# Storing the pieces of x at different places of a 512-byte row, and the first MLP's matmuls in four forms

## The chip, the cores and the metric

The kernel runs on one core of a Trainium2 chip. The metric is the device time of one execution in microseconds (us), lower is better. The kernel before takes 803.97 us, the median of two runs (803.86 and 804.07).

## What is computed

Retention (attention with a decay in place of the softmax) on 4 x 8 heads of 576 tokens, then two MLPs over 2304 tokens, each 512 wide with a hidden width of 2048:

```python
ret = (scale * q @ k.T) * Dmat          # Dmat[i, j] = gamma ** (i - j) for i >= j, else 0
x   = (ret @ v), heads side by side     # 2304 x 512
h   = np.maximum(x @ w_in, 0.0)         # first MLP
x   = h * h @ w_out
h   = x @ w_in2                         # second MLP
out = (h * np.clip(h + 3.0, 0.0, 6.0) / 6.0) @ w_out2
```

## The kernel before

**Stages.** Retention for the first four 128-token chunks comes first. Then the first MLP runs over five blocks of tokens (512, 384, 512, 384, 512), and the rest of retention is done in between its matmuls. Then the second MLP runs in three super-blocks, each with a stage of matmuls 384 columns wide (z, L1183) and one 256 columns wide (z, L1238).

**Precision.** Each fp32 number is held as two fp32r numbers, a high part and a low part, and each product is made of three matmuls (high by high, high by low, low by high). So `x`, `w` and `g` have an axis of 2: index 0 is the high part, index 1 the low one.

**First MLP.** A step is one of the 16 hidden blocks f of 128 in one block of tokens. `h_part` (L623) does 12 matmuls: the stationary operand is a 128 x 128 piece of `w` (part wi, quarter c of the 512 inputs), the moving one the piece `x[:, xi, c, :]` of as many columns as the block has tokens. ACT then makes relu (L632), DVE multiplies it with h (L634), ACT casts the square to g's high part (L636), DVE subtracts for the low part (L642). `a_part` (L660) does 12 matmuls with pieces of `w` as the stationary and `g` as the moving operand. On PE the order is h of step i+1, then retention's small matmuls if any, then acc of step i. In all these are 588 h matmuls for the 512-token blocks (24 of them 256 columns wide, as step 0 is done in halves), 576 acc matmuls for the same blocks, and 384 of each for the 384-token blocks.

**Weights of the first MLP** are brought in and split during the first block of tokens only, and kept. For each f there are two halves (input weights and output weights). `scale_w` on ACT (L140, L141) and `narrow_w` on DVE (L158, L159) work on the raw 64-bit numbers, whose words they read 8 bytes apart. `cast_w` on ACT (L167) writes w's high part, `low_w` on POOL or DVE (L174) the low part. The high parts are read contiguously and written contiguously.

**Where the tiles lie.** The pools are laid out so that every stationary and moving tile of the first MLP, and `xop` and `ring` of the second, starts 160 bytes into a 512-byte row of its partition; a piece of 128 weights is 512 bytes, and a piece of x or g is 2048 or 1536 bytes, so each piece starts there too. The splits `spl`, the stationary operands of L1238, are the only ones elsewhere: five of six tiles start 224 bytes into the row and the sixth 352, against a moving `ring` at 160.

Of the kernel before, what the change touches and what calls it, by code (L numbers as in the profile page):

```python
# [12 lines left out]
F32R = mybir.dt.float32r  # L13
# [6 lines left out]
P = 128  # L20
B, H, S, D = 4, 8, 576, 64
NT = B * S
DM = H * D
DFF = 2048
NPAIR = H // 2
NC = DM // P
# [9 lines left out]
NJ = NF // 2  # L36
# [50 lines left out]
def retention_moe_kernel(ctx: ExitStack, tc, qk, kv, w1, w2, cst, out):  # L87
# [5 lines left out]
    nc = tc.nc  # L93
    nblk = len(BLOCKS)
    start = np.concatenate([[0], np.cumsum([n for n, _ in BLOCKS])]).tolist()

    def pool(stack, name, bufs, **kw):
        return stack.enter_context(tc.tile_pool(name=name, bufs=bufs, reuse_waits="tile", **kw))
# [7 lines left out]
    whi = pool(left, "whi", 1, side="left")  # L106
# [3 lines left out]
    wlo = pool(right, "wlo", 1, side="right")  # L110
# [7 lines left out]
    ctx.enter_context(tc.manual_schedule())  # L118


    raws = {}
    wts = {}
    narrowed = [0]
# [38 lines left out]
    def cast_w(ph, f, halves=(0, 1)):  # L162

        for i in halves:
            t = wts[ph, f, i]
            w = (wlo if f < NJ else whi).tile([P, 2, DM], F32R, tag=f"w{f}_{i}", name=f"w_{ph}_{f}_{i}")
            nc.scalar.activation(w[:, 0, :], t, AF.Copy)  # L167
            wts[ph, f, i] = w, t

# [7 lines left out]
    def split_w(ph, f, halves=(0, 1)):  # L177
        cast_w(ph, f, halves)
        low_w(ph, f, halves)
# [19 lines left out]
    xs = {}  # L199
# [411 lines left out]
    def h_part(ph, blk, f, between=lambda: None):  # L611
        nb = BLOCKS[blk][0]
        w = wts[ph, f, 0]
        x = xs[ph, blk]
        hp = ps_h.tile([P, 512], F32, tag="h", name=f"h_{ph}_{blk}_{f}")
        def order(last):
            return [(c, wi, xi) for wi, xi in ((0, 0), last[::-1], last) for c in range(NC)]

        parts = 2 if ph == blk == f == 0 else 1
        for i in range(parts):  # L620
            ts = slice(i * nb // parts, (i + 1) * nb // parts)
            for k, (c, wi, xi) in enumerate(order((1, 0) if blk == 0 and i == 0 else (0, 1))):
                nc.tensor.matmul(  # L623
                    hp[:, ts],
                    w[:, wi, c * P : (c + 1) * P],
                    x[:, xi, c, ts],
                    start=k == 0,
                    stop=k == 3 * NC - 1,
                )
        r = tmpp.tile([P, 512], F32, tag="tmp", name=f"r_{ph}_{blk}_{f}")  # L630
        r = r[:, :nb]
        nc.scalar.activation(r, hp[:, :nb], AF.Relu)  # L632
        between()
        nc.vector.tensor_tensor(r, r, hp[:, :nb], ALU.mult)  # L634
        g = gpool.tile([P, 2, 512], F32R, tag="g", name=f"g_{ph}_{blk}_{f}")
        nc.scalar.activation(g[:, 0, :nb], r, AF.Copy)  # L636
        gts[ph, blk, f] = g, r
# [7 lines left out]
    def a_part(ph, blk, f):  # L645
        nb = BLOCKS[blk][0]
        w = wts[ph, f, 1]
        g = gts.pop((ph, blk, f))
        if f == 0:
            two = [  # L650
                ps_acc.tile([P, 2, 512], F32, tag="acc", name=f"acc_{ph}_{blk}_{d}")
                for d in range(2)
            ]
            accs[ph, blk] = [two[d // 2][:, d % 2, :] for d in range(NC)]
        acc = accs[ph, blk]
        last = f == NF - 1

        def mm(d, wi, gi, first, stop):
            wt = w[:, wi, d * P : (d + 1) * P]
            nc.tensor.matmul(acc[d][:, :nb], wt, g[:, gi, :nb], start=first, stop=stop)  # L660

        if last:
            for d in range(NC):
                mm(d, 0, 0, False, False)
                mm(d, 1, 0, False, False)
                mm(d, 0, 1, False, True)
        else:
            for d in range(NC):
                mm(d, 0, 0, f == 0, False)
                mm(d, 1, 0, False, False)  # L670
            for d in range(NC):
                mm(d, 0, 1, False, False)
# [23 lines left out]
    def new_x(ph, blk):  # L696
        nb, tag = BLOCKS[blk]
        p = xbpool if tag == "xb" else xapool
        xs[ph, blk] = p.tile([P, 2, NC, nb], F32R, tag=tag, name=f"x_{ph}_{blk}")

# [159 lines left out]
    for f in range(2, 4):  # L862
        load_w(0, f)
    nc.sync.dma_start(con, cst[:, DK0:])
    new_x(0, 0)

    first_q(0, nc.vector)
# [29 lines left out]
    narrow_w(0, 0, (0,))  # L897
    scale_w(0, 1, (0,))
    cast_w(0, 0, (0,))
    first_x(2, low=True)  # L900
    first_values(3)
# [5 lines left out]
    for i in range(2):  # L907
        first_x(3, i, 2, low=True)
    cast_w(0, 1, (0,))
    scale_w(0, 0, (1,))  # L910
    low_w(0, 1, (0,))
# [3 lines left out]
    def early_between():  # L915
        narrow_w(0, 0, (1,))
        split_w(0, 0, (1,))

    h_part(0, 0, 0, early_between)
    narrow_w(0, 2, (0,))  # L920
    g_low(0, 0, 0)
# [44 lines left out]
    for i, (ph, blk, f) in enumerate(steps):  # L966
# [13 lines left out]
        if i + 1 < len(steps):  # L980
            h_part(*steps[i + 1], lambda: first_between(f) if blk == 0 else None)
            if i == 0:
                narrow_w(0, 1, (1,))
            if blk == 0 and f + 1 < NF:
                cast_w(0, f + 1, (1,))
            if i == 0:
                g_low(*steps[1])
                low_w(0, 1, (1,), nc.vector)
                scale_w(0, 3, (0,))
                first_sum(n0 - 1)  # L990
                scale_w(0, 2, (1,))
            if blk == 0 and f:
                scale_ahead(f, False)
# [11 lines left out]
        if blk + 1 < nblk:  # L1005
            if f == 0:
                new_x(0, blk + 1)
# [153 lines left out]
    for s in range(SUPERS):  # L1161
# [8 lines left out]
        for j in range(NJ):  # L1170
# [5 lines left out]
            for i, q in enumerate(ORDER):  # L1176
                run(now)
                w = wring[s, 0, j, i // 2][:, i % 2]
                x = x_ops[q]
                for k, (u, wi, xi) in enumerate(  # L1180
# [6 lines left out]
                        start=k == 0 and q not in (2, 4, 3),  # L1187
                        stop=k == 5,
# [35 lines left out]
        for i, q in enumerate(ORDER):  # L1224
# [7 lines left out]
            for k, parts in work:  # L1232
                run(now)
                w, sp = wring[s, 1, q, k // 2], splits[s, q, k]
                for n in parts:
                    o = z[A_BANKS[q][n // 2]][:, HALFD * (n % 2) : HALFD * (n % 2 + 1)]
                    for m, (g, wi) in enumerate(((0, 0), (0, 1), (1, 0))):
# [4 lines left out]
                            start=k == 0 and m == 0 and n % 2 == 0 and q not in (2, 4, 3),  # L1242
                            stop=k == NJ - 1 and m == 2 and n > 0,
# [49 lines left out]
```

## Time and profile before

| what | value |
|---|---|
| median of the two runs | 803.97 us |
| span of the profiled execution | 802.6 us |
| TensorE (PE) busy | 796.4 us, 99% |
| weight loads (PEld) busy | 741.0 us, 92% |
| VectorE (DVE) busy | 591.9 us, 74% |
| ScalarE (ACT) busy | 397.5 us, 50% |
| GpSimd (POOL) busy | 167.7 us, 21% |
| DMA share | 73.5% of 16 engines |

The profiled execution is known by its span, 802.6 us from its first to its last instruction; the two timed runs are other executions, whose median is 1.4 us above that span. A matmul's duration in the profile holds both its columns and the time until its last result is written, so durations of matmuls in a stream overlap. The time that one costs is the distance between the starts of two that follow each other, called the pitch here.

### The profile page before, as it was taken

To read this page: it belongs to the slowest core of one execution; us is meant where nothing else is said; L and a number is where in the kernel's file an instruction comes from. 1 tells how busy PE (TensorE), PEld (TensorE's weight loads), DVE (VectorE), ACT (ScalarE), POOL (GpSimd) and SP (SyncE) were. 2 spreads that over 40 slices of the span, in tenths; PEclk is the share of its full clock that TensorE was granted. 3 is DMA by queue.
4 is the path that set the end of the run, shared out by engine and by line. 5 is a ranking of instruction groups with operands and counts; after the bars stand their busy time and mean duration, and the time that the engine had idled before them with its cause. 6 is when DMAs were issued, how large, how long until landed. Compare 5 with 4: busy or idle time off the path is not lost.

```text
span 802.6 us, 16522 instructions
## 1 busy us (share of the span) xinstructions
PE 796.4 (99%) x6380; PEld 741.0 (92%) x6380; DVE 591.9 (74%) x1086; ACT 397.5 (50%) x738; POOL 167.7 (21%) x161
## 2 busy tenths in 40 slices
PE   8999999999999999999999999999999999999998
PEld 8788889999888899998888899999999999999998
DVE  5989987887755577776557867997577987677864
ACT  2797745444443444444435533666234655244553
POOL 4412130211011011100000065500255500256300
PEclk9999999999999999999999999999999999999999
DMA  9957626777756487856448797888887979877884
GB/s 331 352 189 248 223 93 203 225 214 222 222 157 184 124 260 212 234 158 184 145 130 269 242 303 256 306 307 291 274 264 242 353 261 302 279 240 266 272 274 139
DMA packets 148494, 189.64 MB, mean 236 GB/s; under 512 B 22592, under 2 KB 102080, under 8 KB 148416
## 3 DMA queue, kind: packets, MB, share of 16 engines
q1 hardware_dynamic: 148416, 188.59, 73.5%
q8 instruction: 50, 0.82, 0.4%
q14 instruction: 28, 0.23, 0.1%
HBM read 149.76 MB, written 38.80 MB: 235 GB/s over the span
## 4 chain that ended last, share of the span: by engine, by line
PE 95%; DMA 3%; DVE 1%; SPq 0%; ACT 0%; issue 0%; DVEq 0%
PE acc L660 24%; PE h L623 24%; PE z L1183 22%; PE z L1238 21%; PE at L496 2%; DMA raw<-w_dram 1%; DMA v<-kv_dram 1%; DMA kv<-kv_dram 1%; PE alone L496 0%; PE sc L408 0%; PE o L459 0%; PE sc L419 0%; DVE wt L158 0%; DVE wt L159 0%; PE o L469 0%; ACT w L167 0%
## 5 line engine op out<-in xcount | busy, mean ns | idle before, releaser
L660 PE MATMUL acc<-g,w 128*128 128x512 f32 (+1 forms) x960 | 213.3, 370 | 0.4 <-ACT g L636 0.4
L623 PE MATMUL h<-x,w 128*128 128x512 f32 (+2 forms) x972 | 210.6, 365 | 0.2 <-ACT w L167 0.2
L660 PEld LDWEIGHTS acc<-g,w 128*128 128x128 f32 x960 | 173.6, 188 | 25.2 <-ACT g L636 0.8
L623 PEld LDWEIGHTS h<-x,w 128*128 128x128 f32 x972 | 175.7, 188 | 22.8 <-ACT w L167 0.6
L1183 PE MATMUL z<-xop,ring 128*128 128x384 f32 x1008 | 175.2, 334 | 0.0
L1183 PEld LDWEIGHTS z<-xop,ring 128*128 128x128 f32 x1008 | 174.7, 188 | 0.1
L1238 PE MATMUL z<-ring,spl 128*128 128x256 f32 x1512 | 172.2, 276 | 0.0
L1238 PEld LDWEIGHTS z<-ring,spl 128*128 128x128 f32 x1512 | 172.1, 188 | 0.0
L1099 POOL TENSOR_TENSOR aop<-aop,aop 128x384 f32<-128x384 f32 x96 | 106.2, 1116 | 296.2 <-DVE aop L1096 292.4
L1121 DVE TENSOR_TENSOR spl<-aop,spl 128x384 fp32r<-128x384 f32 x168 | 100.5, 617 | 30.7 <-ACT spl L1117 29.4
L1117 ACT ACTIVATE spl<-aop 128x384 fp32r<-128x384 f32 x168 | 86.3, 523 | 54.7 <-PE z L1238 49.8
L632 ACT ACTIVATE r<-h 128x512 f32<-128x512 f32 (+1 forms) x80 | 44.3, 553 | 110.7 <-PE h L623 110.4
L1093 ACT ACTIVATE aop<-held,small 128x384 f32<-128x384 f32 x72 | 44.4, 617 | 108.4 <-DVE held L1059 107.8
L634 DVE TENSOR_TENSOR r<-r,h 128x512 f32<-128x512 f32 (+1 forms) x80 | 50.5, 632 | 53.9 <-ACT r L632 53.5
L1059 DVE TENSOR_TENSOR held<-z,held 128x384 f32<-128x384 f32 x120 | 66.4, 553 | 28.9 <-PE z L1183 26.7
L636 ACT ACTIVATE g<-r 128x512 fp32r<-128x512 f32 (+1 forms) x80 | 47.2, 590 | 65.8 <-DVE r L634 65.8
L642 DVE TENSOR_TENSOR g<-r,g 128x512 fp32r<-128x512 f32 (+1 forms) x80 | 54.7, 684 | 21.0 <-ACT g L636 18.5
L1096 DVE SCALAR_TENSOR_TENSOR aop<-aop,held 128x384 f32<-128x384 f32 x72 | 49.9, 692 | 17.7 <-ACT aop L1093 16.1
L393 POOL TENSOR_TENSOR qs<-qs,con 128x512 f32<-128x512 f32 x11 | 14.7, 1340 | 136.3 <-DMA qs<-qk_dram 123.9
L750 ACT ACTIVATE uhi<-seven 128x896 fp32r<-128x896 f32 x32 | 30.6, 955 | 23.7 <-DVE seven L740 14.0
L755 DVE TENSOR_TENSOR seven<-seven,uhi 128x896 fp32r<-128x896 f32 x32 | 34.9, 1089 | 7.3 <-ACT uhi L750 7.0
L174 POOL TENSOR_TENSOR w<-wt,w 128x512 fp32r<-128x512 f32 x17 | 22.7, 1336 | 62.9 <-ACT w L167 60.2
(111 smaller groups left out, 609.8 us busy)
## 6 DMA issues: line engine op xcount, KB each, us to landing
ring<-w_out_hl SPq DMA_DIRECT2D x84, 512.0 KB, 4.9
ring<-w_in_hl SPq DMA_DIRECT2D x72, 512.0 KB, 4.7
raw<-w_dram SPq DMA_DIRECT2D x32, 512.0 KB, 7.1
uraw<-w_dram SPq DMA_DIRECT2D x64, 256.0 KB, 3.2
q<-qk_dram SPq DMA_DIRECT2D x17, 512.0 KB, 5.3
w_in_hl<-uhi SPq DMA_DIRECT2D x16, 448.0 KB, 3.4
w_in_hl<-seven SPq DMA_DIRECT2D x16, 448.0 KB, 4.8
w_out_hl<-uhi SPq DMA_DIRECT2D x16, 448.0 KB, 3.2
```

Source lines behind the costliest of these rows:

```text
L623: nc.tensor.matmul(hp[:, ts], w[:, wi, c * P : (c + 1) * P], x[:, xi, c, ts], start=k == 0, stop=k == 3 * NC - 1,)
L634: nc.vector.tensor_tensor(r, r, hp[:, :nb], ALU.mult)
L636: nc.scalar.activation(g[:, 0, :nb], r, AF.Copy)
L642: nc.vector.tensor_tensor(g[:, 1, :nb], r, g[:, 0, :nb].bitcast(F32), ALU.subtract)
L660: nc.tensor.matmul(acc[d][:, :nb], wt, g[:, gi, :nb], start=first, stop=stop)
L1059: fn(*a)
L1096: stt(f32(q, j), f32(q, j), 6.0, h, ALU.min, ALU.mult)
L1099: nc.gpsimd.tensor_tensor(f32(o, j), f32(a, j), f32(b, j), op)
L1117: act(t[:, 0, :], f32(q, k), AF.Copy)
L1121: tt(t[:, 1, :], f32(q, k), t[:, 0, :].bitcast(F32), ALU.subtract)
L1183: nc.tensor.matmul(bank[q], w[:, wi, u * P : (u + 1) * P], x[:, u, xi, :], start=k == 0 and q not in (2, 4, 3), stop=k == 5, skip_group_ch ...
L1238: nc.tensor.matmul(o, sp[:, g, P * n : P * (n + 1)], w[:, k % 2, wi, :], start=k == 0 and m == 0 and n % 2 == 0 and q not in (2, 4, 3), st ...
```

## The change

Three things, all in the first MLP; the number of instructions, the work of each and their order on each of the five engines stay the same.

- `new_x`: the x tile of a 512-token block gets rows of 528 elements of which 512 are used. Piece (xi, c) then starts 160 + 64 c + 256 xi bytes into the 512-byte row, modulo 512: 160, 224, 288, 352 for the high parts and 416, 480, 32, 96 for the low ones. Of the 12 h matmuls of a step, the two with (xi, c) = (0, 0) still start where their weights do, the other ten don't. The x tiles of 384-token blocks and the g tiles stay. The tiles behind x move by 512 bytes, so their place in the row stays.
- `woven`: for f = 4 to 7 and 12 to 15, w's high and low parts lie alternately, so a part's 128 weights are 8 bytes apart and span 1024 bytes. The cast, the subtraction and the weight loads of these f work with that step.
- `backwards`: for f = 2, 3, 6, 7, 10, 11, 14, 15, the moving operand is read from its last column to its first, in both `h_part` and `a_part`: h comes out with its tokens in reverse, g inherits that, and the second reversal puts acc right.

So four f each are plain (0, 1, 8, 9), backwards (2, 3, 10, 11), woven (4, 5, 12, 13), and both (6, 7, 14, 15).

```diff
+    def woven(f):
+        return f // 4 % 2 == 1
+
+    def backwards(f):
+        return f // 2 % 2 == 1
+
+    def turned(ap, yes):
+        return ap[:, ::-1] if yes else ap
...
-            w = (wlo if f < NJ else whi).tile([P, 2, DM], F32R, tag=f"w{f}_{i}", name=f"w_{ph}_{f}_{i}")
+            p, name = wlo if f < NJ else whi, f"w_{ph}_{f}_{i}"
+            if woven(f):
+                w = p.tile([P, DM, 2], F32R, tag=f"w{f}_{i}", name=name).rearrange("p n t -> p t n")
+            else:
+                w = p.tile([P, 2, DM], F32R, tag=f"w{f}_{i}", name=name)
...
-                    x[:, xi, c, ts],
+                    turned(x[:, xi, c, ts], backwards(f)),
...
-            nc.tensor.matmul(acc[d][:, :nb], wt, g[:, gi, :nb], start=first, stop=stop)
+            gt = turned(g[:, gi, :nb], backwards(f))
+            nc.tensor.matmul(acc[d][:, :nb], wt, gt, start=first, stop=stop)
...
-        xs[ph, blk] = p.tile([P, 2, NC, nb], F32R, tag=tag, name=f"x_{ph}_{blk}")
+        step = nb + 16 * (tag == "xa")
+        x = p.tile([P, 2, NC, step], F32R, tag=tag, name=f"x_{ph}_{blk}")
+        xs[ph, blk] = x[:, :, :, :nb]
```

## Rows read from the trace of the kernel before

**Rows 1.** The page: busy time and share of PE; its granted clock by slice.
```profile
PE 796.4 (99%) x6380; PEld 741.0 (92%) x6380; DVE 591.9 (74%) x1086; ACT 397.5 (50%) x738; POOL 167.7 (21%) x161
...
PEclk9999999999999999999999999999999999999999
```

**Rows 2.** The page: the chain that ended last, shares by engine.
```profile
PE 95%; DMA 3%; DVE 1%; SPq 0%; ACT 0%; issue 0%; DVEq 0%
```

**Rows 3.** Waits of PE: who waited for whom, us in total, times, longest.
```profile
PE unread L851 <- POOL early L845: 1.0, 1, 1.0
...
PE h L623 <- ACT w L167: 0.2, 1, 0.2
```

**Rows 4.** Groups by shape: line, engine, tiles, shapes, count | busy us, mean ns.
```profile
L1238 PE MATMUL z<-ring,spl 128*128 128x256 f32 x1512 | 172.2, 276 | 0.0
L660 PE MATMUL acc<-g,w 128*128 128x512 f32 x576 | 140.4, 392 | 0.4 <-ACT g L636 0.4
L623 PE MATMUL h<-x,w 128*128 128x512 f32 x564 | 135.8, 390 | 0.2 <-ACT w L167 0.2
L660 PE MATMUL acc<-g,w 128*128 128x384 f32 x384 | 72.9, 337 | 0.0
L623 PE MATMUL h<-x,w 128*128 128x384 f32 x384 | 71.8, 334 | 0.0
```

**Rows 5.** Timeline of PE in steady stretches: start us, length us, matmuls merged.
```profile
215.44 2.88 PE L660 MATMUL acc<-g,w 128*128 128x512 f32 x12
218.16 2.88 PE L623 MATMUL h<-x,w 128*128 128x512 f32 x12
...
125.13 2.24 PE L660 MATMUL acc<-g,w 128*128 128x384 f32 x12
127.21 2.25 PE L623 MATMUL h<-x,w 128*128 128x384 f32 x12
```

**Rows 6.** Timeline of PE: two stretches of 256-wide matmuls.
```profile
22.91 2.92 PE L623 MATMUL h<-x,w 128*128 128x256 f32 x23
...
529.80 15.46 PE L1238 MATMUL z<-ring,spl 128*128 128x256 f32 x135
```

**Rows 7.** One matmul and one weight load in 23.1:25.6; mean ns last.
```profile
L623 PE MATMUL h<-x,w 128*128 128x256 f32 x23 | 2.9, 283 | 0.0
...
L623 PEld LDWEIGHTS h<-x,w 128*128 128x128 f32 x23 | 2.8, 192 | 0.0
```

**Rows 8.** Weight loads by shape, whole span, 128 and 64 columns wide.
```profile
L1238 PEld LDWEIGHTS z<-ring,spl 128*128 128x128 f32 x1512 | 172.1, 188 | 0.0
L496 PEld LDWEIGHTS alone<-p,v 64*64 64x64 f32 x176 | 6.0, 135 | 0.0
```

**Rows 9.** Groups by shape on ACT, DVE and POOL: the weights' preparation.
```profile
L140 ACT ACTIVATE raw<-raw 128x512 f32<-128x512 f32 x32 | 21.3, 666 | 1.0 <-DMA raw<-w_dram 1.0
L167 ACT ACTIVATE w<-wt 128x512 fp32r<-128x512 f32 x32 | 19.9, 623 | 4.0 <-DVE wt L159 3.9
...
L642 DVE TENSOR_TENSOR g<-r,g 128x512 fp32r<-128x512 f32 x48 | 34.5, 719 | 11.6 <-ACT g L636 9.1 <-PE alone L496 1.4 <-PE at L496 0.7
L174 DVE TENSOR_TENSOR w<-wt,w 128x512 fp32r<-128x512 f32 x15 | 11.1, 740 | 0.1
...
L174 POOL TENSOR_TENSOR w<-wt,w 128x512 fp32r<-128x512 f32 x17 | 22.7, 1336 | 62.9 <-ACT w L167 60.2 <-issue 2.7
```

**Rows 10.** Timeline of the first block around one step's weights, several engines.
```profile
96.48 2.88 PE L660 MATMUL acc<-g,w 128*128 128x512 f32 x12
...
97.17 0.62 ACT L167 ACTIVATE w<-wt 128x512 fp32r<-128x512 f32 x1
...
97.87 1.30 POOL L174 TENSOR_TENSOR w<-wt,w 128x512 fp32r<-128x512 f32 x1 [5.04 <-ACT w L167]
...
99.20 2.88 PE L623 MATMUL h<-x,w 128*128 128x512 f32 x12
...
100.45 0.68 DVE L174 TENSOR_TENSOR w<-wt,w 128x512 fp32r<-128x512 f32 x1
...
103.10 0.50 PE L660 MATMUL acc<-g,w 128*128 128x512 f32 x1
```

**Rows 11.** Busy time by stretch, first block: us, PE, PEld, DVE, ACT, POOL.
```profile
36.00:118.00 82.00, 81.80 (x737) 66.34 (x736) 72.68 (x126) 61.57 (x112) 21.76 (x18) 1.00 0.60 202
```

## Prediction

> **What bounds the kernel now.** I read the page's busy shares first, then the chain, then PE's waits, to see whether anything but PE counts. [...] The chain that ended last is PE's for 95% [rows 2]. PE's longest wait is 1.0 us and its shortest listed 0.2 us, six waits in all, 2.7 us together [rows 3]. So the time is the number of matmuls times the pitch of one, and an edit counts only if it changes a pitch or makes PE wait.
>
> So I read the pitches in steady stretches. For 512 columns, twelve acc matmuls start at 215.44 and the h matmuls behind them at 218.16 [rows 5]: 2.72 / 12 = 0.2267 us. The columns alone, at 2.4 GHz, are 512 / 2.4 = 213.3 ns, so 13.3 ns are lost per matmul. For 384 columns it is (127.21 - 125.13) / 12 = 173.3 ns [rows 5] against 160.0: again 13.3 ns. The loss does not depend on the width, so it belongs to the change from one matmul to the next.
>
> The rows that matter most are two stretches of the same shape, 128 x 128 weights against 256 columns [rows 6]. From a stretch I take off the last matmul's own duration, 283 or 276 ns [rows 7, 4], and divide by the starts that are left. In the first block, L623: (2.92 - 0.283) / 22 = 119.9 ns. In the second MLP, L1238: (15.46 - 0.276) / 134 = 113.3 ns. The columns are 106.7 ns in both, so one loses 13.2 and the other 6.6. A weight load lasts 192 ns in the first and 188 in the second [rows 7, 8]. What differs between the two in the kernel is the place in the 512-byte row: in L623 weights and moving operand start at the same byte, in L1238 64 or 192 bytes apart. That is what the change tries on h. The trace does not prove that the place is the cause, since the two lines also write PSUM differently, but every matmul of the first MLP, whose tiles lie at many different places and have only the place in the row in common, has the 13.3 ns.
>
> **The change, part by part.**
>
> *x's pieces.* It touches 564 + 24 = 588 h matmuls [rows 4] (the 24 are in the first step), of which 10 in 12 = 490 no longer start where their weights do. The saving of one lies between nothing and 13.3 ns, all that a 512-column matmul loses. I take 6.6 ns, the difference of the two 256-wide stretches, since it is the only row of before with starts apart. 490 x 0.0066 = 3.2 us; the bounds are 0 and 6.5 us. A loss is not excluded either, as only distances of 64 and 192 bytes have a row and the change makes seven; I bound it by the same 3.2 us the other way.
>
> [...]
>
> *Backwards.* 960 matmuls: 288 h and 288 acc of 512 columns, 192 and 192 of 384. No row shows an operand read backwards. The bounds are a loss of 13.3 ns that vanishes (12.8 us gained) and columns at half speed (below). I take nothing: the same bytes are read, and the row's traffic is the same. *Woven.* Also 960 matmuls, half of which are backwards too. The weight loads read 8 bytes apart, which no row shows on PE either. A load takes 188 ns for 128 columns and 135 for 64 [rows 8], so 53 for 64 columns, 0.83 ns each, and 106.7 for 128; the rest is latency. It lies beside a matmul whose pitch is 227 or 173 ns, so a load that is no more than 1.5 times as slow costs nothing. I take nothing, with bounds from 12.8 us gained to the rival below.
>
> *Preparing woven weights,* first block only. 16 casts on ACT and 16 subtractions on POOL and DVE write (and read) 8 bytes apart. For ACT the near rows are L140, which reads and writes at that step, 666 ns, against L167's 623 [rows 9]: 16 x 43 ns = 0.7 us on an engine that is busy 61.6 of 82 us there [rows 11]. For L174 no row has the step with two inputs; between no change and a doubling I take no change. What hides it: the POOL subtraction ends at 97.87 + 1.30 = 99.17, and the h step that starts at 99.20 wants the low weights only in its last four matmuls, 8 x 0.227 = 1.8 us later; the DVE one ends at 101.13 and its acc step starts at 103.10 [rows 10]. A doubled subtraction (1.3 and 0.7 us more) still fits. Queued behind on DVE are the next narrowings, and DVE is busy 72.7 of 82 us [rows 11]; 8 x 0.7 = 5.6 us more would fit there too, with PE waits of a few tenths.
>
> *Nothing is moved:* each engine's instructions stand in the order of before, and no wait is added.
>
> **Sum.** The profiled span 802.6 - 3.2 = 799.4 us; with the 1.4 us that the median of the runs lies above it, 800.8 us. [...]
>
> **Rivals.**
>
> *The forms shed the loss too.* If what costs is that both streams go through the row in step, then any form that breaks the step saves 6.6 ns in the matmuls without an offset: in three forms of four, 432 + 288 acc, 288 h of 384 columns and 72 h of 512, 1080 x 0.0066 = 7.1 us more: 793.7. For it: the loss is the same in all plain matmuls with equal starts. Against it: nothing shows which direction or step would help.
>
> *The forms make it worse by one meeting.* Streams that run against each other meet more often. One more loss of 6.6 ns in the 960 backward matmuls is 6.3 us: 807.1. No row speaks for or against.
>
> *The change does nothing,* 804.0: the loss is a fixed cost of changing weights, and L1238 is shorter for another reason. For it: 13.3 ns at 512 and 384 columns alike. Against it: the 256-wide stretches. [...]
>
> *Woven loads at half speed.* A load would read for 213 ns instead of 107, and with the 6.6 ns between loads of L1238 no matmul could follow another in under 220 ns. 512-column matmuls at 226.7 hide that; 384-column ones at 173.3 don't: half of 768 x 46.6 ns = 17.9 us, and about 1 us where a load follows a wait and is not hidden: 800.8 + 18.9 = 819.7. It decides from the point where a load takes 173 ns or more to read. [...]
>
> *Backward columns at half speed,* the slower side. Place: the moving operand of 960 matmuls on PE. Price: 576 x 213.3 + 384 x 160.0 ns = 184 us, 985 us. It passes 2% (16.1 us, beyond the 3.2 gained) once a backward matmul takes 20 ns longer. For it: no moving operand of before runs backwards. Against it: only the direction changes, the numbers read and their places are the same.
>
> **Chances.** Offset helps, forms neutral: 0.42. Forms shed the loss too: 0.13. Forms worse by one meeting: 0.15. Nothing: 0.12. Woven loads slow: 0.10. Backward slow: 0.08. The predicted time is that of the likeliest, 800.8 us; its own range is 797 to 804, from the bounds of x's pieces (6.5 and 0 us). The whole range is 793 to 821, from the forms that shed to the slow woven loads; it leaves out the slow columns (0.08) and tails of the others, some 0.15. About 2% is what a measurement of this kernel can tell from no change. Faster by over 2%, under 787.9, needs nearly all of the loss gone in the forms: 0.04, out of the second case. Slower by over 2%, over 820.0: the slow columns (0.08), half of the slow loads, which end close to that bound (0.05), and 0.04 for meetings that cost several times 6.6 ns: 0.17. Within 2%: 0.79.
>
> **What would show it.** Pitches by step in a 512-token block: plain h steps at about 12 x 0.221 = 2.66 us in place of 2.72, acc steps of f = 0, 1, 8, 9 still 2.72. For each form, the acc steps and the 384-column steps tell its own price without x's offset. Woven loads at half speed would show as weight loads near 295 ns in place of 188; slow columns as durations near 600 ns in place of 390. If h steps of all f stay at 2.72, x's pieces do nothing. The forecast is wrong if any form moves the pitch of its acc steps by more than about 7 ns either way, or if PE's waits in the first block grow beyond a microsecond.

## The result and the profile after

The changed kernel takes 812.49 us (two runs, 812.38 and 812.60) against 803.97: a ratio of 1.0107, with a 95% interval of 1.0077 to 1.0136. It is slower, where 800.8 us and a small gain were forecast; it lies within the 2% that most of the chance was on. The profiled execution's span is 810.6 us against 802.6, 8.0 us more.

The page after, parts 1 and 2, which answer to [rows 1]:

```profile
PE 803.7 (99%) x6380; PEld 747.1 (92%) x6380; DVE 591.9 (73%) x1086; ACT 399.7 (49%) x738; POOL 169.3 (21%) x161
...
PEclk9999999999999999999999999999999999999999
```

PE is as full as before and its clock as high, so the time has not gone into waiting or into the clock: PE is busy 7.3 us longer with the same 6380 matmuls. The groups by shape on PE and its weight loads, after (columns as in [rows 4]); h is now L636, acc L674, and the second MLP's stages are L1199 and L1254:

```profile
L1199 PE MATMUL z<-xop,ring 128*128 128x384 f32 x1008 | 175.2, 334 | 0.0
L1254 PE MATMUL z<-ring,spl 128*128 128x256 f32 x1512 | 172.2, 276 | 0.0
L674 PE MATMUL acc<-g,w 128*128 128x512 f32 x576 | 143.2, 398 | 0.4 <-ACT g L649 0.4
L636 PE MATMUL h<-x,w 128*128 128x512 f32 x564 | 139.0, 396 | 0.2 <-ACT w L180 0.2
L674 PE MATMUL acc<-g,w 128*128 128x384 f32 x384 | 73.6, 341 | 0.0
L636 PE MATMUL h<-x,w 128*128 128x384 f32 x384 | 72.7, 338 | 0.0
...
L636 PEld LDWEIGHTS h<-x,w 128*128 128x128 f32 x972 | 178.7, 192 | 23.7 <-ACT w L180 0.6
```

Beside [rows 4], acc of 512 columns went from 140.4 to 143.2 us, h from 135.8 to 139.0, acc of 384 from 72.9 to 73.6 and h from 71.8 to 72.7. That is 2.8 + 3.2 + 0.7 + 0.9 = 7.6 of the 8.0 us. The second MLP, which the change doesn't touch, is the same to a tenth. Weight loads last 192 ns in the mean against 188; those of woven f last 195 ns and none over 201, so none is at half speed.

The steps one by one, in the chain of work of the third block (512 columns); columns are start us, length us, and 12 matmuls of a step. They are h of f = 3 (backwards), acc of f = 2, h of f = 4 (woven), and further down h of f = 9, acc of f = 8 and acc of f = 9, all plain:

```profile
216.06 2.80 PE h L636 x12
218.87 2.80 PE acc L674 x12
221.67 2.78 PE h L636 x12
...
251.86 2.79 PE h L636 x12
254.64 2.73 PE acc L674 x12
...
260.18 2.77 PE acc L674 x12
```

Before, each such step was 2.72 us [rows 5]. Only the plain acc steps, whose code is that of before, still come close: 2.73 behind a plain h step, 2.77 behind a backward one. A plain h step, which has nothing new but x's offset, takes 2.79 in place of the 2.66 that was forecast: 232.5 ns per matmul, not 221. A backward acc step, which has no offset, takes 2.80: 233.3 ns.

### The profile page after: what moved, and what is told of

Read it like the earlier page. It is cut to its first block, busy times and chain, and to the rows that moved or that the text cites. A ratio compares the mean times of both kernels' runs of the same rounds, so it can differ in the third digit from the quotient of the medians.

```text
span 810.6 us, 16522 instructions
## 1 busy us (share of the span) xinstructions
PE 803.7 (99%) x6380; PEld 747.1 (92%) x6380; DVE 591.9 (73%) x1086; ACT 399.7 (49%) x738; POOL 169.3 (21%) x161
## 4 chain that ended last, share of the span: by engine, by line
PE 95%; DMA 2%; DVE 2%; ACT 1%; issue 0%; SPq 0%; POOL 0%; DVEq 0%; POOLq 0%
PE acc L674 25%; PE h L636 24%; PE z L1199 22%; PE z L1254 21%; PE at L509 2%; DMA q<-qk_dram 2%; DVE wt L167 1%; PE alone L509 0%; DVE wt L168 0%; PE sc L421 0%; ACT w L180 0%; PE o L472 0%; PE sc L432 0%; SPq L243 0%; PE o L482 0%
## 5 line engine op out<-in xcount | busy, mean ns | idle before, releaser
L674 PE MATMUL acc<-g,w 128*128 128x512 f32 (+1 forms) x960 | 216.8, 375 | 0.4 <-ACT g L649 0.4
L636 PE MATMUL h<-x,w 128*128 128x512 f32 (+2 forms) x972 | 214.7, 370 | 0.2 <-ACT w L180 0.2
L636 PEld LDWEIGHTS h<-x,w 128*128 128x128 f32 x972 | 178.7, 192 | 23.7 <-ACT w L180 0.6
L674 PEld LDWEIGHTS acc<-g,w 128*128 128x128 f32 x960 | 176.8, 192 | 25.4 <-ACT g L649 0.8
L1199 PE MATMUL z<-xop,ring 128*128 128x384 f32 x1008 | 175.2, 334 | 0.0
L1199 PEld LDWEIGHTS z<-xop,ring 128*128 128x128 f32 x1008 | 174.7, 188 | 0.1
L1254 PE MATMUL z<-ring,spl 128*128 128x256 f32 x1512 | 172.2, 276 | 0.0
L1254 PEld LDWEIGHTS z<-ring,spl 128*128 128x128 f32 x1512 | 172.1, 188 | 0.0
L1115 POOL TENSOR_TENSOR aop<-aop,aop 128x384 f32<-128x384 f32 x96 | 108.0, 1135 | 296.7 <-DVE aop L1112 292.9
L1137 DVE TENSOR_TENSOR spl<-aop,spl 128x384 fp32r<-128x384 f32 x168 | 98.6, 604 | 31.1 <-ACT spl L1133 29.0
```

The costliest lines, as they stand in the source:

```text
L636: nc.tensor.matmul(hp[:, ts], w[:, wi, c * P : (c + 1) * P], turned(x[:, xi, c, ts], backwards(f)), start=k == 0, stop=k == 3 * NC - 1,)
L674: nc.tensor.matmul(acc[d][:, :nb], wt, gt, start=first, stop=stop)
L1115: nc.gpsimd.tensor_tensor(f32(o, j), f32(a, j), f32(b, j), op)
L1137: tt(t[:, 1, :], f32(q, k), t[:, 0, :].bitcast(F32), ALU.subtract)
L1199: nc.tensor.matmul(bank[q], w[:, wi, u * P : (u + 1) * P], x[:, u, xi, :], start=k == 0 and q not in (2, 4, 3), stop=k == 5, skip_group_ch ...
L1254: nc.tensor.matmul(o, sp[:, g, P * n : P * (n + 1)], w[:, k % 2, wi, :], start=k == 0 and m == 0 and n % 2 == 0 and q not in (2, 4, 3), st ...
```

## The experiments

Times are medians, set against the kernel before on the same chip (804.4 to 804.5 us; the two runs of the last part are single executions, read for their pitches alone). A pitch is the length of a stretch in the chain of work divided by its matmuls.

### Each part alone

The theory that the profile after suggests: a stream of wide matmuls has one state that repeats from matmul to matmul at 13.3 ns above its columns, and each of the three parts breaks it by itself. "State" is a name for what the starts show, and for nothing inside the engine. The columns are counted here and below at 2.4 to a ns, an estimate from [rows 5]: 128 columns more take 226.7 - 173.3 = 53.4 ns. The rival: the offset saves as forecast, and the parts only cost together.

**The offset alone.** The diff is that of `new_x` in the change, without the rest.

> The kernel before with the x tiles of the 512-token blocks in rows of 528 alone: no f is read backwards, no weights are woven. In the changed kernel the plain h steps of 512 columns went from 226.7 to about 232.5 ns per matmul. Theory A, unequal starts of the moving pieces are by themselves a loss: all 588 h matmuls at 231 to 234 ns, acc and 384-column matmuls as before, time about 804.0 + 588 x 0.0055 = 807.2 us. Theory B, the offset saves 6.6 ns each as predicted and the forms beside it spoiled the plain steps: h at about 221 ns, 800.8 us.

Measured: 807.84 us, a ratio of 1.0044 (1.0029 to 1.0059), 3.5 us slower. The chain in the third block:

```profile
228.12 2.74 PE acc L660 x12
230.86 2.79 PE h L623 x12
```

The h steps are at 2.79 us, and the acc steps, which are untouched, come to 2.74, 0.02 above before. The offset is a loss of some 6 ns per matmul where a gain of 6.6 was forecast.

**Backwards alone.** With `backwards` and `turned` of the change:

```diff
-                    x[:, xi, c, ts],
+                    turned(x[:, xi, c, ts], backwards(f)),
...
-            nc.tensor.matmul(acc[d][:, :nb], wt, g[:, gi, :nb], start=first, stop=stop)
+            gt = turned(g[:, gi, :nb], backwards(f))
+            nc.tensor.matmul(acc[d][:, :nb], wt, gt, start=first, stop=stop)
```

> The kernel before with the moving operands of f = 2, 3, 6, 7, 10, 11, 14, 15 read backwards alone: x's rows stay 512 long, no weights are woven. Theory A, a backward stream costs by itself: as in the changed kernel, 576 matmuls of 512 columns at about 233 ns (3.6 us) and 384 of 384 columns at about 178 ns (1.7 us), 809.3 us. Theory B, the forms cost only through x's offset: 804 us.

Measured: 809.88 us, 1.0067 (1.0052 to 1.0082), 5.5 us slower. The chain where the second block (384 columns) goes over into the third; h is L632, acc L670:

```profile
194.66 2.13 PE acc L670 x12
196.79 2.73 PE h L632 x12
...
204.40 2.72 PE acc L670 x12
207.12 2.80 PE h L632 x12
```

The first row is acc of f = 14, backwards, 384 columns: 2.13 us in place of 2.08 (4.3 ns per matmul in the mean of such steps). The next are 512 columns: h and acc of f = 0, both forward, at 2.73 and 2.72, and the first backward one, h of f = 2, at 2.80.

**Woven alone.** With `woven` of the change:

```diff
-            w = (wlo if f < NJ else whi).tile([P, 2, DM], F32R, tag=f"w{f}_{i}", name=f"w_{ph}_{f}_{i}")
+            p, name = wlo if f < NJ else whi, f"w_{ph}_{f}_{i}"
+            if woven(f):
+                w = p.tile([P, DM, 2], F32R, tag=f"w{f}_{i}", name=name).rearrange("p n t -> p t n")
+            else:
+                w = p.tile([P, 2, DM], F32R, tag=f"w{f}_{i}", name=name)
```

> The kernel before with the weights of f = 4 to 7 and 12 to 15 woven alone. Theory A, the step of 8 bytes costs by itself but only beside 512 columns: 576 matmuls at about 233 ns, the 384-column ones at 173.3, 804.0 + 3.6 = 807.6 us; the sum of the three parts alone is then larger than the changed kernel's 8.5 us, since the forms overlap. Theory B, it costs nothing without x's offset: 804 us.

Measured: 808.17 us, 1.0045 (1.0028 to 1.0061), 3.8 us slower. The chain in the third block, acc of f = 2 (plain) and h of f = 4 (woven):

```profile
217.06 2.72 PE acc L673 x12
219.79 2.80 PE h L636 x12
```

576 matmuls of 512 columns at 2.80 / 12 = 233.3 ns are 576 x 6.7 = 3.8 us, all of it; the groups of 384 columns stay as before (72.0 and 72.8 us busy).

The three losses sum to 12.8 us and the change costs 8.5. That fits parts that break the same state: an h matmul that has the offset and goes backwards pays some 6 ns once, not twice. In the change 588 h and 432 acc matmuls of 512 columns are out of the state, 1020 x 6 ns = 6.1 us, and 384 backward ones of 384 columns, 384 x 4.3 ns = 1.7 us: 7.8 us. The 72 plain acc matmuls of f = 1 and 9, whose steps stand behind a backward h step, add 72 x 4 ns = 0.3 us.

### Was the place of the splits the cause of the 113.4 ns?

```diff
-    SHIFT, FIRST_SHIFT = 64 // 4, 192 // 4
+    SHIFT, FIRST_SHIFT = 512 // 4, 0
...
-    p1a.tile([P, 128 - SHIFT], F32, tag="shift1", name="shift1")
```

> The kernel before with the splits of the second MLP, the stationary operands of its 256-column matmuls, at the same place of the 512-byte row as the moving ring tiles (160) in place of 224 and 352. Theory A, which the prediction rested on, that the distance of the starts sets the loss: 1512 matmuls go from 113.4 to 119.9 ns, 804.0 + 10 = 814 us. Theory B, the 113.4 ns belongs to that stage for another reason: 804 us.

Measured: 813.92 us, 1.0119 (1.0104 to 1.0134), 9.5 us slower. Pieces of the chain, whole stages of the second MLP's first super-block. Before:

```profile
452.82 58.27 PE z L1183 x336
511.09 57.18 PE z L1238 x504
```

In this run:

```profile
452.61 58.26 PE z L1183 x336
510.87 60.47 PE z L1238 x504
```

60.47 / 504 = 120.0 ns, where the stage had 57.18 / 504 = 113.5. So the inference from [rows 6] held: in the 256-column stage the place of the stationary operand sets the loss, and this alone is worth 9.5 us. In this run nothing but the place of the splits was changed, and each matmul takes 6.5 ns longer. Whether the load takes reads from the matmul, this run doesn't tell.

### Does a constant distance help wide matmuls?

The offset gave x's pieces seven distances in turn. Two runs give the first MLP's weights one constant distance instead, by a tile of padding ahead of them (the first run's edit; the second has 448 and 256 in place of 192 and 64):

```diff
+    whi.tile([P, 192 // 4], F32, tag="whi_shift", name="whi_shift")
...
+    wlo.tile([P, 64 // 4], F32, tag="wlo_shift", name="wlo_shift")
```

> The kernel before with the first MLP's weights moved within the 512-byte row, x and g left at 160: weights of f = 0 to 7 start 64 bytes later (224), those of f = 8 to 15 192 bytes later (352), the two distances that the second MLP's 256-column stage has. Every matmul of the first MLP has then unequal but constant starts. Theory A, what counts is that starts are constant from matmul to matmul, and a distance of 64 or 192 then saves: 512 columns at about 220 ns, 384 at about 167, 1932 x 6.6 ns = 12.8 us less, 791 us. Theory B, equal starts are the best state for wide matmuls and the distance helps only at 256 columns, where the weight loads fill the whole pitch: 512 columns at 231 to 234 ns, about 804 + 1140 x 0.006 = 811 us or more.

> As the run before it, with weights of f = 0 to 7 256 bytes later in the row than x and g, and of f = 8 to 15 448 bytes later (64 earlier). Theory A, any constant distance saves: 791 us. Theory B, equal starts are best for wide matmuls: 811 us or more. If one half of the f shows another pitch than the other, the distance itself matters, and which one is read from the stretches.

Measured: 808.63 us (1.0051, 1.0031 to 1.0071) with 64 and 192 bytes; 805.78 us (1.0014, 1.0004 to 1.0024) with 256 and 448. The chain in the third block, first with 64 bytes (f under 8), then 192:

```profile
228.35 2.80 PE acc L663 x12
...
263.86 2.75 PE acc L663 x12
```

and with 256 bytes, then 448:

```profile
227.69 2.72 PE acc L663 x12
...
262.75 2.75 PE acc L663 x12
```

So 233.3 ns at 64 bytes, 229.2 at 192 and 448, and 226.7, the value of equal starts, at 256. No distance gets below equal starts, so theory A falls in both runs. Theory B has the direction right but its 811 us is too much, as it put the same loss on every distance. In the 384-column blocks of both runs the distances cost next to nothing: the 768 matmuls are busy 145.3 and 144.7 us, where they were 144.7 before [rows 4]. Nor does a distance of 64 bytes help in the second MLP's 384-column stage, where xop was moved by a padding tile ahead of it:

```diff
+        p.tile([P, 448 // 4], F32, tag="xshift", name="xshift")
         for q in ORDER:
             x_ops[q] = p.tile([P, 2, 2, HALF], F32R, tag=f"x{q}", name=f"xop_{q}")
+        p.tile([P, (512 - 448) // 4], F32, tag="xrest", name="xrest")
```

> The kernel before with xop, the moving operand of the second MLP's 384-column stage, 64 bytes earlier in the row than ring, its stationary operand (96 against 160), the same distance as in the 256-column stage. Theory A, a constant distance saves there too: 1008 matmuls from 173.3 to 166.7 ns, 797.3 us. Theory B, equal starts are the best state for matmuls wider than 256 columns: 173.3 stays or rises by some 4 ns, as it did for backward ones, 804 to 809 us.

Measured: 805.98 us, 1.0017 (1.0007 to 1.0027). That stage, L1185 here:

```profile
452.73 58.69 PE z L1185 x336
```

58.69 / 336 = 174.7 ns, in place of 58.27 / 336 = 173.4. Two things are told apart with that: it is not the change of distance from piece to piece alone that costs, since constant ones cost too; and the gain from a distance of 64 bytes belongs to 256 columns.

Does the place itself count, apart from the distance? All tiles 32 bytes later:

```diff
+    cpool.tile([P, 8], F32, tag="by32", name="by32")
...
-    pool(ctx, "align", 1, side="right").tile([P, 80], F32, tag="align", name="align")
+    pool(ctx, "align", 1, side="right").tile([P, 72], F32, tag="align", name="align")
```

> The kernel before with all tiles on both sides 32 bytes later, so that the streams start at 192 in place of 160 bytes into the 512-byte row, a multiple of 64; all distances stay. Theory A, only distances count: 804 us with every pitch as before. Theory B, the 13.3 ns is partly a piece of 64 bytes that is begun in its middle: the pitches of 512 and 384 columns fall by 6.7 ns or less, down to about 787 us with the second MLP's 384-column stage.

Measured: 804.44 us, 1.0002 (0.9992 to 1.0012), and the steps of 512 columns stay at 2.72 us. So moving everything by 32 bytes changes nothing; with what stands above, the distance counts and the place, as far as tried, does not.

And is it 256 bytes that the places repeat by? x's low parts 256 bytes further, so that the moving starts change within each h step:

```diff
-        xs[ph, blk] = p.tile([P, 2, NC, nb], F32R, tag=tag, name=f"x_{ph}_{blk}")
+        rest = 64 * (tag == "xa")
+        x = p.tile([P, 2, NC * nb + rest], F32R, tag=tag, name=f"x_{ph}_{blk}")
+        xs[ph, blk] = x[:, :, : NC * nb].rearrange("p t (c n) -> p t c n", c=NC)
```

> The kernel before with the low parts of x in the 512-token blocks 256 bytes further in the row than the high parts (416 against 160), nothing else: the starts of h's moving pieces change within a step, as in the change, but by 256 bytes in place of 64. Theory A, places count modulo 256 bytes: h stays at 226.7 ns and the time at 804 us. Theory B, any change of place from one moving piece to the next spoils the repeating state: h at 231 to 234 ns in part of its matmuls, 805 to 807 us.

Measured: 804.35 us, 0.9998 (0.9989 to 1.0008). The same kind of edit as the change's, with 256 bytes in place of 64, costs nothing; h and acc in the third block:

```profile
224.07 2.72 PE h L623 x12
226.79 2.72 PE acc L660 x12
```

So of the ten matmuls in twelve that no longer start where their weights do, the one with (xi, c) = (1, 0), 256 bytes off, counts as not moved.

### The matmul by itself

Two runs carry a tail of stretches of 48 matmuls, each with one thing changed. In the tails DVE, ACT and POOL do nothing, DMA's share is 0.00 and the granted clock 1.00. For instance, weights 64 bytes further (`cut` takes a tile, the byte to start at, the step in elements and the number of elements):

```diff
+    for k in range(48):  # d64
+        nc.tensor.matmul(z[5 - k % 2][:128, :512], cut(pw, 64, 1, 128), cut(px[k % 2], 0 + 0 * k % 512, 1, 512), start=True, stop=True)
```

> The kernel before with a tail that measures: behind the second MLP, 25 stretches of 48 matmuls each on tiles of xop, one thing changed at a time, their sums read by nobody (the tail adds some 260 us and is no part of what is computed). Base: 512 columns, 128 weights, equal starts. Theory A, the loss comes from the weight load's reads meeting the moving operand's: it follows the number of weights, 13.3 ns with 128, about 6.7 with 64 and 3.3 with 32, and the start distances and directions change it as in the stages (starts 64 or 192 bytes apart: 229 to 234 ns in place of 226.7; 256 apart: 226.7; moving backwards and woven weights: 233; moving pieces that go on by 64 bytes each: 232; 256 columns: 120 with equal starts, 113.3 with 64 apart). Theory B, it is a fixed price of changing the weights: 13.3 ns with 64 and 32 weights too.

> The kernel before with another tail of 26 stretches of 48 matmuls whose sums nobody reads (some 280 us, no part of what is computed). It asks three things. First, whether the backward stretch's 233.3 ns at 512 columns is its direction or its place, since reading from the last column starts 4 bytes short of the weights' place. Theory A, the place: backward from byte 2048 of the tile (equal places) gives 226.7 ns, and forward with weights 4 or 252 bytes off gives about 233. Theory B, the direction: backward gives about 233 from every start, and 4 bytes forward change nothing. Second, why 256 columns with starts 64 bytes apart give 113.4 ns in the second MLP and 117.7 in the tail of the run before: if the PSUM bank is what differs, 256 columns into one bank, or three in a row into each, give 113.3 and alternating banks 117.7; if the moving tile is, one tile in place of two gives 113.3. Third, whether the loss is 13.3 ns for widths that are no multiple of 128: 504, 496, 480, 448 and 416 columns at N / 2.4 + 13.3, that is 223.3, 220.0, 213.3, 200.0 and 186.7 ns, or more where such a width spoils the repeating state.

The first tail's chain; columns are start us, length us, line, and 48 matmuls. In order: equal starts, 64 weights, 32 weights, distances of 16, (32 left out, 11.20,) 64, 128, 192, 256 bytes (those of 320, 384 and 448, L1285 to L1289, are left out: 11.20, 11.16 and 10.99), backwards, woven. A distance is how far the weights start behind the moving operand:

```profile
803.33 10.98 PE z L1267 x48
814.31 11.04 PE z L1269 x48
825.35 11.12 PE z L1271 x48
836.47 11.20 PE z L1273 x48
...
858.87 11.20 PE z L1277 x48
870.07 11.15 PE z L1279 x48
881.22 10.99 PE z L1281 x48
892.21 10.88 PE z L1283 x48
...
936.45 11.20 PE z L1291 x48
947.64 11.20 PE z L1293 x48
958.84 11.28 PE z L1295 x48
970.12 21.75 PE z L1297 x48
991.87 11.13 PE z L1299 x48
1003.00 10.89 PE z L1301 x48
1013.90 5.75 PE z L1303 x48
...
1025.30 5.45 PE z L1307 x48
...
1055.92 10.89 PE z L1315 x48
```

L1295 is weights 16 bytes apart, L1297 moving numbers 8 bytes apart, L1299 moving pieces that go on by 64 bytes, L1301 by 256. L1303 is 256 columns with equal starts, L1307 the same with 64 weights, and L1315 is the first form once more. The second tail's chain: L1281 is the backward stretch that starts at the weights' place (four others are left out, 11.31 each), L1291 to L1295 are 496, 480 and 504 columns, L1309 is 256 columns with the weights 64 bytes off and one moving tile:

```profile
880.41 11.30 PE z L1281 x48
...
936.94 10.72 PE z L1291 x48
947.66 10.41 PE z L1293 x48
958.08 10.88 PE z L1295 x48
...
1009.94 5.44 PE z L1309 x48
```

Divided by 48, in ns per matmul of 512 columns unless said:

| what is changed | pitch | over the columns |
|---|---|---|
| equal starts (L1315); 256 bytes apart; pieces that go on by 256 | 226.7 to 226.9 | 13.3 to 13.5 |
| 192 or 448 apart | 229.0 | 15.7 |
| 240, 8 and 96 apart (second tail: 10.97, 11.07 and 11.24 us) | 228.5, 230.6, 234.2 | 15.2, 17.3, 20.8 |
| 4 apart (L1269 of the second tail, 11.16 us) | 232.5 | 19.2 |
| 128 or 384 apart; pieces that go on by 64 | 231.9 to 232.5 | 18.6 to 19.2 |
| 16, 32, 64, 224, 252 or 320 apart; backwards from 4 bytes short; woven | 233.3 | 20.0 |
| backwards from the weights' place and four other starts | 235.4 to 235.6 | 22 |
| weights with a step of 16 bytes | 235.0 | 21.7 |
| 64 weights, 32 weights, equal starts | 230.0, 231.7 | 16.7, 18.3 |
| 504, 496, 480 columns, equal starts | 226.7, 223.3, 216.9 | 16.7, 16.6, 16.9 |
| 448, 416 columns, equal starts (9.72 and 9.04 us) | 202.5, 188.3 | 15.8, 15.0 |
| 384 columns: equal starts; 64 weights; backwards (8.32, 8.32, 8.53 us) | 173.3, 173.3, 177.7 | 13.3, 13.3, 17.7 |
| 256 columns, equal starts: 128 weights; 64 weights | 119.8, 113.5 | 13.1, 6.9 |
| 256 columns, 64 or 192 apart; 32 apart, two moving tiles (5.65, 5.68 us) | 117.7, 118.3 | 11.0, 11.7 |
| 256 columns, 64 bytes apart, one moving tile | 113.3 | 6.7 |

The first stretch, L1267, has equal starts and yet 10.98 / 48 = 228.8 ns. In the trace the first ten distances from one start to the next are 224 to 285 ns and those from the eleventh on 226 to 228, so the stretch's own pitch is that of L1315.

Three readings. First, the stages' numbers come back without any other engine's work beside them, so ACT, DVE, POOL and DMA have no part in this. Second, both theories of the first tail fall at 512 columns: the loss neither follows the number of weights nor stays at 13.3 ns. With half or a quarter of them it is larger, 230.0 and 231.7 ns, so there it is not time that the weight load takes from the matmul piece by piece. At 384 columns 64 weights change nothing, and at 256 they make the matmul 6.3 ns shorter, as theory A has it; for that width it is not refuted. What is special at 512 columns, among the forms tried, are equal starts with 128 weights: in the trace such a stretch, once it has settled, has its starts 226 to 228 ns apart, where that with 64 weights goes 236, 229, 224, 227, 234, 230 and round again. The five widths that are no multiple of 128 columns lose 15.0 to 16.9 ns with equal starts, more than 512 and 384 do. Third, the backward loss is the direction's: from a start equal to the weights' place it is 235.4 ns, no better than the 233.3 of the start 4 bytes short, so theory A of the second tail falls. Theory B falls in its other half, as 4 bytes forward do cost (232.5 ns): direction and place each cost by themselves. The same goes for the woven weights, whose low parts also start 4 bytes off: the tail's woven stretch starts at an equal place and has 233.3 ns, so the step is enough.

A constant distance explains only part of the offset's price. Twelve matmuls at the tail's pitches for the change's distances, three each at 0, 64, 128 and 192 bytes modulo 256, would have (226.7 + 233.3 + 232.4 + 229.0) / 4 = 230.4 ns in the mean, an estimate from these rows; the h steps measured 232.5. So the change from piece to piece seems to cost some 2 ns more, which was not followed up.

On the 256-column question: one moving tile gives 113.3 ns with alternating PSUM banks too, and the first tail's 117.7 came from two moving tiles in turn, both at the same place of the row. So the PSUM bank is not what differs; why two tiles in turn cost 4.4 ns there, and nothing at 512 columns with equal starts, was not followed up.

## Why the prediction was wrong, point by point

- **What bounds the kernel** held: PE is 99% busy before and after, and 7.6 of 8.0 us are in its pitches. No row gives the clock in GHz: the 2.4 GHz by which the forecast takes off the columns is the rate that [rows 5] show, 128 / 53.4 = 2.4 columns a ns. The 0.4 us left is of the size by which PE's listed waits grew (2.7 to 3.6 us in all, the growth at retention's first chunks, ahead of any changed work).
- **x's pieces, -3.2 us**: the step that failed first. The sum took the 6.6 ns that separate two 256-column stretches [rows 6] and gave them to 512-column matmuls. The place is the cause at 256 columns, which the run with equal splits shows, but at 512 columns equal starts are the best of all distances tried, and at 384 none of those tried is better. The term was +3.5 us. Its far bound below nothing, a loss of 3.2 us, was about the truth and was taken for the less likely side. The sentence ahead of it went wrong first: the same 13.3 ns at 512 and 384 columns was read as a price of changing over, from which a part could be taken away, when it is what the repeating state gives; a row of another distance at 512 columns is what was missing.
- **The forms, 0 us**: the other term that failed, and nearly as large. Of the 11.7 us between 800.8 and 812.49, x's term has 6.7 (from -3.2 to +3.5); the other 5.0 came from the two forms, which were put at nothing and took the change from 3.5 to 8.5 us.
- **Backwards, 0 us**: +5.5 us alone. The reason given (the same bytes are read) was no evidence on time. The rival of "one meeting", 6.6 ns in each of 960 matmuls, came near in size: 6.7 ns at 512 columns, 4.3 at 384. Its picture, streams that meet more often, is not shown by any run.
- **Woven, 0 us**: +3.8 us alone, all at 512 columns; at 384 it is nothing. The reason given was that a load which lasts little longer is hidden beside the matmul. The loads did last little longer (195 ns for 188 in the change, 193 in the tail's woven stretch), less than the 226.7 ns from one matmul to the next, and each 512-column matmul still took 6.7 ns more: that a load fits beside the matmul doesn't make its form free.
- **Preparation of the woven weights** at nothing: right. The casts go from 623 to 652 ns in the mean, the subtractions from 740 to 685 on DVE, and no wait of PE names them beyond the 0.2 us of before [rows 3].
- **The slow rivals** fell for this change, but their prices exist one step further on. The tail's weight loads with a step of 16 bytes last 310 ns, where those of woven weights, with a step of 8, last 193. A moving operand with a step of 8 bytes takes 21.75 / 48 = 453 ns, half the speed of the 226.7 ns with equal starts.
- **What would show it** worked in part: the forecast named plain h steps at 2.66 us, and 2.79 refuted it in one row. But the sign set for the forms, 7 ns in their acc steps, was too wide: 6.7 ns passed under it and cost 3.8 us and more for each form.

The range of the likeliest case, 797 to 804 us, missed. The whole range, 793 to 821 us, held the time by luck: its upper end was the price of slow woven loads, which did not come. That about 2% is the least that can be told here was also too coarse: the interval of 1.0077 to 1.0136 is clear of no change. No version was found that beats the kernel before: of all distances, directions, steps and widths tried, none gives a 512- or 384-column matmul less than the 13.3 ns that it has.

## What to carry to other kernels

A difference between two rows is a price only for the shape at which both were read: before it is carried to a wider matmul, measure that width, which a tail of 48 matmuls per question does in 11 us each. By these runs, streams of fp32r matmuls with a weight load each do best with stationary and moving operands at equal places modulo 256 bytes when they are 512 columns wide (226.7 against 228.5 to 234.2 ns), and with a distance of 64 bytes when they are 256 wide (113.4 against 120.0); at 384 columns a distance of 64 bytes costs 1.3 ns (174.7 against 173.4). Several edits that break the same state cost once, so their prices alone do not add (12.8 against 8.5 us).

## What was not expected of the hardware

- At 512 columns the place of an operand counts modulo 256 bytes, not 512: 64 and 320, 128 and 384, 192 and 448 bytes give the same pitch to 0.2 ns (233.3, 232.3 to 232.5 and 229.0 ns in the first tail).
- At 512 columns fewer weights make a matmul longer (230.0 ns with 64 against 226.7 with 128), where at 256 columns they make it shorter (113.5 against 119.8). 504 columns take as long as 512, 226.7 ns.
- After a break the stream needs some matmuls to find its state again. In the kernel before, the step behind the retention matmuls at 109.93 us lasts 2.95 us and the next 2.72:

```profile
109.93 2.95 PE acc L660 x12
112.88 2.72 PE h L623 x12
```

  In the trace the second start of that step lies 339 ns behind the first, the next five 229 to 236 ns apart, and then all 226 or 227. In the first tail it took ten matmuls.

- What makes the state repeat, and why at 256 bytes, stays open: no run here looks inside it.
